# Issuing the second of two output stores from ScalarE's queue instead of SyncE's

## The chip, the core and the metric

The kernel runs on one core of one Trainium2 chip. A core has TensorE (PE), VectorE (DVE), ScalarE (ACT), GpSimd (POOL) and SyncE (SP), and 16 DMA engines that all issuing queues share. The metric is the device time of one execution in microseconds (us), given as the median of several runs. The profile of one execution has its own clock, the span, which is about 1.7 us shorter than the device time. Times "at" some point are counted from the start of the span. The issue of a DMA is the time that its DMA instruction takes on an engine's queue; its landing is the last of the semaphore updates (a semaphore is a counter by which one unit tells another that something is done) that tell of its completion. All runs compared here are of the fast state, with a granted TensorE clock of 0.996 to 1.0.

## The reference

It is one block of grouped-query attention with a K and V cache, followed by the output projection:

```python
B, Sq, D = 32, 4, 1024
Hq, Hkv, Sk, Dh = 32, 4, 2048, 128
q = (x @ wq).reshape(B, Sq, Hq, Dh).transpose(0, 2, 1, 3)
k = repeat(k_cache, Hq // Hkv, axis=1); v = repeat(v_cache, Hq // Hkv, axis=1)
p = softmax(einsum("bhqd,bhkd->bhqk", q, k) * Dh ** -0.5)
o = einsum("bhqk,bhkd->bhqd", p, v)
y = o.transpose(0, 2, 1, 3).reshape(B, Sq, Hq * Dh) @ wo      # all bf16
```

The output y is 128 rows (B times Sq) of 1024 bf16 values, 256 KB. The inputs are 151 MB, 134 MB of them K and V.

## The kernel before

SyncE issues every load, far ahead. The last inputs to arrive are pieces of wo. TensorE multiplies with them into three column ranges of y in PSUM. VectorE and ScalarE evict these ranges to SBUF (the array `y_sb`), and two DMAs of 128 KB store the halves of y.

```python
NA = 512
NB = 800
COLS = ((0, 0, NA), (512, NA, NB), (1024, NB, D))      # (column in PSUM, first, last column of y)
# ... cut ...
        def oproj_out():
            def copy(eng, at, n0, n1, j):
                dst, src = y_sb[:, n0:n1], ps_s[:, at:at + n1 - n0]
                # ScalarE: activation(Copy), VectorE: tensor_copy; both wait for ("op", j), signal ("oe", j)
                # ... cut ...
            for j, eng in enumerate(("dve", "act", "dve")):
                copy(eng, *COLS[j], j)
            for j, (n0, n1, waits) in enumerate(((0, NA, (0,)), (NA, D, (1, 2)))):
                p.dma("sp", lambda e, n0=n0, n1=n1: e.dma_start(out_flat[:, n0:n1], y_sb[:, n0:n1]),
                      [("oe", i) for i in waits], ("out", j), f"s_o{j}")
# ... cut: the projection's matmuls; oproj_out() comes last ...
        p.op("sp", lambda e: None, [("out", j) for j in range(2)])     # SyncE waits for both stores
```

Store 1 (columns 0 to 512) needs VectorE's first eviction. Store 2 (columns 512 to 1024) needs ScalarE's eviction (512 to 800) and VectorE's second (800 to 1024). The first load of the program is x, and the loads of wq follow it on the same queue:

```python
        p.dma("sp", lambda e: e.dma_start(x_sb, x_flat[:, :]), [], "x", "s_x")
        for c in range(4):
            p.dma("sp", ...  w_sb[:, 2 * c:2 * c + 2, :] <- wq_v ...)
```

## Time and profile before

| | |
|---|---|
| device time, median of 3 runs | 363.12 us (363.08 to 363.22) |
| span of the profiled run | 361.4 us |
| busy share: PE, DVE, ACT | 85%, 75%, 28% |
| DMA over the span | 420 GB/s |

The first fence is from the page of the kernel before: in 40 equal slices of the span, the busy tenths of the 16 DMA engines and what they moved.

```profile
DMA  8999999999999999999999999999999999999995
GB/s 321 433 435 432 424 424 428 435 423 424 423 428 432 428 424 430 431 430 426 424 433 428 425 428 430 430 428 426 428 432 432 426 423 435 428 426 428 413 415 215
```

The DMA engines are at nine tenths or more from the second slice to the last but one. The loads set the pace, and the engines fall idle only at the two ends.

The second fence is the timeline of the last microseconds before the change (start, duration, engine, line, operation, tiles, count; in brackets the idle time before it and its releaser). SPq is SyncE's queue issuing a DMA.

```profile
358.04 1.04 DVE L434 CAST P_sb<-ps_s 128x512 bf16<-128x512 f32 x2 [15.34 <-PE ps_s L420]
...
358.59 0.41 ACT L432 ACTIVATE P_sb<-ps_s 128x288 bf16<-128x288 f32 x1 [16.23 <-PE ps_s L420]
358.76 0.82 SPq L439 DMA_DIRECT2D out_dram<-P_sb  x2
```

VectorE's two evictions are merged into one line, and so are SyncE's two issues. (P_sb is the memory that `y_sb` lives in.) The trace's record of the single issues gives their durations, 0.347 and 0.356 us:

```profile
L439 SPq DMA_DIRECT2D out_dram<-P_sb x2: 347/352/356, 358.8 to 359.2; - x2
```

The view of DMA busy share by window shows what the stores do to the engines (columns: busy of PE, PEld, DVE, ACT and POOL, the granted clock, DMA share, GB/s). The window is from the first packet of store 1 to the last of store 2:

```profile
359.60:360.62 1.02, 0.00 (x0) 0.00 (x0) 0.00 (x0) 0.00 (x0) 0.00 (x0) 1.00 0.77 257
```

In the last 3.4 us, no packet of a load runs any more (the last ended 0.29 us before the first eviction began). In these the data of store 2 become ready at 359.093 (semaphore records), and SyncE issues it at 359.225, after store 1.

### The profile page before, as it was taken

How to read it: one execution, taken by the hardware profiler on the slowest of the kernel's cores; microseconds unless marked ns; L12 is line 12 of the kernel's file. 1: busy time of each engine (PE TensorE's matmuls, PEld its weight loads, DVE VectorE, ACT ScalarE, POOL GpSimd, SP SyncE). 2: the span in 40 equal slices, each digit the busy share in tenths (PEclk: the TensorE clock that was granted, in tenths of full speed). 3: DMA queues.
4: the chain of work that ended last, by engine and by line, in shares of the span. 5: the costliest groups of instructions: out<-in, count | busy, mean ns of one | idle time of the engine just before them, and what ended most of it. 6: DMA issues, size and time to landing. Idle time of an engine off the chain costs nothing. (4 is left out here: it accounts for less than half of the span.)

```text
span 361.4 us, 6252 instructions
## 1 busy us (share of the span) xinstructions
PE 307.8 (85%) x3034; PEld 147.0 (41%) x2340; DVE 269.4 (75%) x171; ACT 102.6 (28%) x110; POOL 165.4 (46%) x262
## 2 busy tenths in 40 slices
PE   1988788999989999988999888888888898889896
PEld 1002000444444555444444444443333444449711
DVE  0018799999899888879999888888888888866501
ACT  1014222333333333333333333323222233333000
POOL 8002055255555555554455444445555554444000
PEclk9999999999999999999999999999999999999999
DMA  8999999999999999999999999999999999999995
GB/s 321 433 435 432 424 424 428 435 423 424 423 428 432 428 424 430 431 430 426 424 433 428 425 428 430 430 428 426 428 432 432 426 423 435 428 426 428 413 415 215
DMA packets 12251, 151.66 MB, mean 420 GB/s; under 512 B 1360, under 2 KB 2128, under 8 KB 2768
## 3 DMA queue, kind: packets, MB, share of 16 engines
q1 hardware_dynamic: 12240, 151.52, 99.0%
q8 instruction: 6, 0.10, 0.1%
q14 instruction: 5, 0.04, 0.0%
HBM read 151.26 MB, written 0.26 MB: 419 GB/s over the span
## 5 line engine op out<-in xcount | busy, mean ns | idle before, releaser
L328 DVE STREAM_TRANSPOSE KT_sb<-big 128x2048 f32<-128x2048 f32 x64 | 146.6, 2293 | 16.7 <-DMA big<-in_k_cache_dram 16.7
L354 ACT ACTIVATE P_sb<-ps_s,negmx 128x2048 bf16<-128x2048 f32 x32 | 82.1, 2565 | 185.0 <-DVE negmx L350 185.0
L16 PE MATMUL ps_s<-KT_sb,QD_sb 128*128 128x512 bf16 x384 | 103.7, 377 | 0.0
L385 POOL COPY PD_sb<-PT_sb 32x1024 f32<-32x1024 f32 x62 | 64.1, 1034 | 63.3 <-PE ps_r L394 60.4
L385 POOL COPY big<-PT_sb 32x1024 f32<-32x1024 f32 x61 | 63.1, 1034 | 59.1 <-PE ps_r L394 56.3
L350 DVE TENSOR_REDUCE negmx<-ps_s 128x1 f32<-128x2048 f32 x32 | 73.2, 2286 | 12.4 <-PE ps_s L16 10.7
L394 PE MATMUL ps_r<-big 128*128 128x128 bf16 x1024 | 59.8, 219 | 11.4 <-PEq L85 11.4
L394 PE MATMUL ps_r<-big,PD_sb 128*128 128x128 bf16 x1024 | 59.8, 219 | 9.9 <-PEq L85 9.8
L394 PEld LDWEIGHTS ps_r<-big 128*128 128x128 bf16 x1024 | 57.9, 98 | 22.1 <-issue 21.6
L394 PEld LDWEIGHTS ps_r<-big,PD_sb 128*128 128x128 bf16 x1024 | 58.0, 98 | 21.1 <-issue 20.6
L341 PE MATMUL ps_s<-KT_sb,QD_sb 128*128 128x512 bf16 x128 | 48.3, 377 | 18.4 <-PEq L85 18.4
L341 PEld LDWEIGHTS ps_s<-KT_sb,QD_sb 128*128 128x128 bf16 x128 | 12.3, 96 | 103.1 <-issue 103.1
L363 DVE STREAM_TRANSPOSE PT_sb<-P_sb 128x1024 f32<-128x1024 f32 x32 | 39.8, 1245 | 15.8 <-ACT P_sb L354 15.8
L318 POOL COPY QD_sb<-QT_sb 32x64 f32<-32x64 f32 x128 | 29.4, 230 | 46.2 <-DVE QT_sb L297 20.5
L16 PE MATMUL ps_r<-ident 128*128 128x384 bf16 x173 | 33.3, 325 | 0.0
L366 PEld LDWEIGHTS ps_r<-ssum,permf 128*128 128x128 f32 x64 | 11.9, 187 | 24.8 <-issue 23.1
L403 ACT ACTIVATE QT_sb<-ps_r,rinv 128x128 bf16<-128x128 f32 x32 | 11.8, 367 | 29.4 <-PE ps_r L394 27.2
L279 DVE TENSOR_SCALAR KT_sb<-ps_r 128x512 bf16<-128x512 f32 x2 | 1.3, 684 | 20.3 <-PE ps_r L263 20.3
L420 PE MATMUL ps_s<-big,KT_sb 128*128 128x512 bf16 (+1 forms) x34 | 12.5, 375 | 2.0 <-DMA big<-in_wo_dram 1.2
L434 DVE CAST P_sb<-ps_s 128x512 bf16<-128x512 f32 (+1 forms) x2 | 1.0, 542 | 15.3 <-PE ps_s L420 15.3
L16 PE MATMUL ps_s<-big,KT_sb 128*128 128x224 bf16 (+1 forms) x62 | 12.0, 272 | 0.0
L252 PE MATMUL ps_r<-ident 128*128 128x384 bf16 x32 | 10.3, 322 | 0.0
(41 smaller groups left out, 85.8 us busy)
## 6 DMA issues: line engine op xcount, KB each, us to landing
big<-in_k_cache_dram SPq DMA_DIRECT2D x32, 2048.0 KB, 18.6
big<-in_v_cache_dram SPq DMA_DIRECT2D x32, 2048.0 KB, 22.1
big<-in_wq_dram SPq DMA_DIRECT2D x4, 2048.0 KB, 14.0
big<-in_wo_dram SPq DMA_DIRECT2D x6, 1024.0 KB, 22.8
big<-in_wo_dram SPq DMA_DIRECT2D x2, 512.0 KB, 24.3
big<-in_wo_dram SPq DMA_DIRECT2D x2, 256.0 KB, 22.6
big<-in_wo_dram SPq DMA_DIRECT2D x4, 128.0 KB, 17.5
P_sb<-in_x_dram SPq DMA_DIRECT2D x1, 256.0 KB, 2.6
```

The lines of the kernel that those rows point to most:

```text
L16: return eng.add_instruction(mybir.InstMatmult(name=nc.get_next_instruction_name(), engine=eng.engine, start_tensor_calc=start, stop_tenso ...
L318: p.op("pool", lambda e, s=src, d=dst: e.tensor_copy(d, s), waits if g == 0 else [("pt", i - 2)] * (g == 1 and i > 1), ("qd", i) if g == G ...
L328: p.op("dve", lambda e, s=src, d=dst: e.transpose(d, s), waits, ("kt", i, c), gives="t_kt" if c else None)
L341: mm = lambda e, a_=(out_, lhsT, rhs), f=first, l=last: e.matmul(a_[0], lhsT=a_[1], rhs=a_[2], start=f, stop=l, skip_group_check=True)
L350: p.op("dve", lambda e: e.tensor_reduce(negmx[:, i % 4:i % 4 + 1], ps_s[:, :], AX.X, ALU.max, negate=True), [("qk", i)], ("negmx", i))
L354: p.op("act", lambda e: e.activation(P_sb[:, :, :, :].rearrange("p t r w -> p t w r"), ps_s[:, :].rearrange("p (t w r) -> p t w r", w=2, r=R),
L363: p.op("dve", lambda e: e.transpose(dst, src), [("exp", i)], ("pt", i))
L366: p.op("pe", lambda e: e.matmul(ring[(i if i == L else i // 2 * 2) % 4][:, 510 + i % 2:511 + i % 2], lhsT=permf[:, :], rhs=ssum[:, i % 4:i ...
L385: p.op("dve" if i >= B - 2 and g < i - B + 4 else "pool", lambda e, s=src, d=dst: e.tensor_copy(d, s), [free] * (g == 0 or i >= B - 2) + [ ...
L394: p.op("pe", lambda e: e.matmul(buf[:, 0:Dh], lhsT=pd_of(i)[:, t // 2, :, :, :, t % 2].rearrange("p x g q -> p (x g q)"), rhs=big[:, slot_ ...
L403: p.op("act", lambda e: e.activation(dst, src, ACT.Copy, scale=rinv[:, i % 4:i % 4 + 1]), [("pv", i), ("rinv", i)], ("o", i))
L420: mm = lambda e, a=(out_, lhsT, rhs): e.matmul(a[0], lhsT=a[1], rhs=a[2], start=(u == 0), stop=(u == Hq - 1), skip_group_check=True)
```

## The change

The intent is that SyncE's queue need not finish issuing store 1 before store 2 goes out: ScalarE, which has nothing left to do, issues store 2.

```diff
             for j, (n0, n1, waits) in enumerate(((0, NA, (0,)), (NA, D, (1, 2)))):
-                p.dma("sp", lambda e, n0=n0, n1=n1: e.dma_start(out_flat[:, n0:n1], y_sb[:, n0:n1]),
+                p.dma(("sp", "act")[j], lambda e, n0=n0, n1=n1: e.dma_start(out_flat[:, n0:n1], y_sb[:, n0:n1]),
                       [("oe", i) for i in waits], ("out", j), f"s_o{j}")
```

## The prediction

> **What bounds the kernel.** The page's row of the slices has DMA busy at 9 tenths in all 40 slices but the first and the last, at 421 to 435 GB/s through the middle, while VectorE is busy 75%, ScalarE 28%. Loads of K, V and wo set the pace; after them comes a serial tail. The chain of waits puts 27.84 us on the wo loads, then matmuls, then VectorE's two evictions (358.04, 1.04 us for both). The change touches only what follows them, some 2.6 us of 361.4 (0.7%). SyncE loses one DMA instruction, ScalarE gains it as its last; no other engine's order changes.
>
> **The tail in the trace before** (timeline and semaphore records, us from the span's start): VectorE's first eviction 358.04 to 358.73; SyncE issues store 1 at 358.757 for 0.347; ScalarE's eviction of columns 512 to 800 signals at 359.015; VectorE's second eviction (columns 800 to 1024, 0.392 us) signals at 359.093. SyncE is still issuing store 1 until 359.104, takes its wait at 359.156 and issues store 2 at 359.225 for 0.356. Packets of store 1 run 359.605 to 360.12, those of store 2 360.085 to 360.61; the landings are complete at 360.476 and 360.965; SyncE leaves its wait at 360.98; the closing barrier takes the rest, to 361.41.
>
> **What the change costs and saves.** Removed from SyncE: one issue of 0.356 us. Added on ScalarE: the same issue, which I estimate at the same 0.35 us from SyncE's 0.347 and 0.356. ScalarE is idle after 359.01. But the 0.356 is not the gain: the data of store 2 are only ready at 359.093, eleven ns before SyncE is done with store 1. Estimate: the wait instruction passes 0.017 us after the signal (as SyncE's did) and the DMA starts 0.069 us after that (359.156 to 359.225 in the trace), so about 359.18 instead of 359.225. The gain is about 0.045 us, all on the last chain, if the path from issue to landing stays at the 1.74 us of store 2. The Trainium skill, "DMA: Bandwidth & Descriptors", section "Issuing engines are not separate DMA queues", says that issuing from several engines only saves the sequencer's time to initiate; the trace agrees as far as it goes: both stores' packets keep the engines at 0.66 to 0.97 busy from 359.75 to 360.5.
>
> Possible costs: this would be ScalarE's first DMA issue in the program, and a second queue with packets of its own. "Perfetto Trace Analysis", section "DMA Instruction — HWDGE (DVE, Sync)", describes a lock on the descriptor generator, waited for inside the profiled issue; store 1's issue is over by 359.104, so I expect no collision. A dearer first issue, or a slower start on a cold queue, would outweigh the gain; SyncE's own first issue took 0.38 us, so I expect little.
>
> **Prediction.** 363.08 us, range 362.6 to 363.9 (wider upwards for the cold queue). Faster by over 2%: 0.005; within 2%: 0.985; slower by over 2%: 0.01.
>
> **What would show each step.** The timeline of SyncE shows one store, ScalarE's shows the other, starting at 359.15 to 359.22 relative to the same evictions, 0.33 to 0.40 us long; a second queue appears among the DMA queues with 128 data packets of 1 KB; the gap from ScalarE's issue to landing is 1.6 to 1.8 us; the last landing to the span's end stays 0.45 us.
>
> **What would make it wrong.** An issue on ScalarE longer than 0.45 us; a first packet on the new queue more than 0.5 us after the issue ends; a longer closing barrier or start because of the second queue; or an overlap of the two stores that stretches both.

## The result, and the profile after

The changed kernel took 363.05 us (median of 6 runs, 362.96 to 363.14). The kernel before took 363.13 us (6 runs, 363.01 to 363.27). The ratio is 0.9997 with a 95% interval of 0.9984 to 1.001. A ratio is the mean time of one kernel's fast runs over that of the other's of the same rounds, so it is not quite the ratio of the medians.

The timeline of the end after the change:

```profile
357.81 1.05 DVE L434 CAST P_sb<-ps_s 128x512 bf16<-128x512 f32 x2 [15.19 <-PE ps_s L420]
...
358.38 0.41 ACT L432 ACTIVATE P_sb<-ps_s 128x288 bf16<-128x288 f32 x1 [16.09 <-PE ps_s L420]
358.53 0.35 SPq L439 DMA_DIRECT2D out_dram<-P_sb  x1
358.95 0.37 ACTq L439 DMA_DIRECT2D out_dram<-P_sb  x1
```

One store is now on ScalarE's queue (ACTq). Its issue lasts 0.37 us, not 0.35. The records of the two issues, and the window from the first packet of store 1 to the last of store 2, are these:

```profile
L439 SPq DMA_DIRECT2D out_dram<-P_sb x1: 348/348/348, 358.5 to 358.5; - x1
L439 ACTq DMA_DIRECT2D out_dram<-P_sb x1: 373/373/373, 359.0 to 359.0; - x1
```

```profile
359.38:360.37 0.99, 0.00 (x0) 0.00 (x0) 0.00 (x0) 0.00 (x0) 0.00 (x0) 1.00 0.79 265
```

On the page after the change the DMA queues have a new member, q10, which holds 144 packets; by the packet records 128 are of data, 1 KB each, and 16 are of 4 bytes:

```profile
q1 hardware_dynamic: 12096, 151.39, 99.0%
...
q10 hardware_dynamic: 144, 0.13, 0.1%
```

The two profiles' spans differ by 0.236 us (361.414 and 361.178), but the first eviction of y already starts 0.225 us earlier in the second one (357.813 instead of 358.038), in work that the change does not touch. That part is not the change's: over all the profiles whose program is the same up to that point, it starts anywhere from 357.74 to 358.32. Therefore the table counts from the start of VectorE's first eviction. The numbers are from the instruction, semaphore and landing records of the traces; "same_kernel" and "again" are further profiles of the kernel before and of the changed kernel.

| us after the start of the first eviction | before | same_kernel | after | again |
|---|---|---|---|---|
| issue of store 1 starts | 0.719 | 0.719 | 0.719 | 0.719 |
| VectorE's second eviction signals | 1.055 | 1.063 | 1.062 | 1.062 |
| issue of store 2 starts | 1.187 | 1.188 | 1.139 | 1.138 |
| duration of that issue | 0.356 | 0.355 | 0.373 | 0.373 |
| from that start to the landing | 1.740 | 1.742 | 1.770 | 1.774 |
| from the landing to the end | 0.449 | 0.450 | 0.456 | 0.456 |
| end of the span | 3.376 | 3.380 | 3.365 | 3.368 |

Store 2 is issued 0.05 us earlier, takes 0.03 us longer to land, and the span closes 0.006 us later after that. What is left is about 0.01 us.

The packet records show where the 0.03 us are spent. From ScalarE's issue of store 2 to its first packet it took 0.895 and 0.893 us (after, again). SyncE's issue of store 2, where its packets can be told apart because store 1 is on another queue, took 0.864, 0.864 and 0.877 us (swap, best and tail_best below). From the first packet to the end of the last it took 0.52 us on ScalarE's queue, and 0.52 to 0.54 on SyncE's; from there to the landing 0.35 us on both. So the loss lies between the start of the issue and the first packet, and most of it is the issue itself (0.373 us; 0.348 for SyncE's issue in swap).

### The profile page after: what moved, and what is told of

The parts are those of the page before. It is cut to its first block, busy times and chain, and to the rows that moved or that the text cites. A ratio compares the mean times of both kernels' runs of the same rounds, so it can differ in the third digit from the quotient of the medians.

```text
span 361.2 us, 6248 instructions
## 1 busy us (share of the span) xinstructions
PE 307.2 (85%) x3030; PEld 147.0 (41%) x2340; DVE 269.4 (75%) x171; ACT 102.6 (28%) x110; POOL 165.4 (46%) x262
```

## The experiments

Four explanations were at stake.

- Theory 1, readiness: store 2 can't go before its data are ready, so moving it saves only the small hold-up behind store 1.
- Rival 2: a slow first use of ScalarE's queue swallows a larger gain.
- Rival 3: the DMA engines' own work on the two stores binds, whoever issues.
- Rival 4: the two issuing queues share one descriptor generator, so one waits for the other.

In the diffs of swap, many_sp and ready_sp the lines taken out are those of the changed kernel; in x_act_only and tail_best they are those of the kernel before. Each call also ran the kernel before on the same chip. Two of its runs were odd (365.55 and 364.61 us) and widen the intervals of the ratios, so differences of 0.1 us are not decided by times; medians are quoted, and the short distances are read from the profiles.

| run | median us | before, same call | first eviction to end, us |
|---|---|---|---|
| again | 363.01 | 363.12 | 3.368 |
| swap | 363.04 | 363.12 | 3.341 |
| many_sp | 366.14 | 363.12 | 6.395 |
| many_act | 364.59 | 363.12 | 4.863 |
| ready_sp | 363.11 | 363.17 | 3.385 |
| ready_act | 363.02 | 363.17 | 3.283 |
| x_act_only | 363.28 | 363.17 | 3.379 |
| best | 363.14 | 363.17 | 3.304 |
| same_kernel | 363.15 | 363.13 | 3.380 |
| tail_best | 363.13 | 363.13 | 3.309 |

### again: the changed kernel once more

There is no edit.

> The changed kernel once more. From the start of VectorE's first eviction of y to the end of the span it took 3.365 us, against 3.376 before the change. Theory 1 (readiness: store 2 may go only when VectorE's second eviction signals, and SyncE was held up only some 0.05 us longer than that) expects the same again, 3.34 to 3.39 us, and a time within 0.15 us of before. Rival 2 (a slow first issue on ScalarE's queue swallows a larger gain) expects ScalarE's issue to landing clearly longer than SyncE's 1.74 us, over 1.9.

It measured 3.368 us, as the first profile's 3.365, and ScalarE's issue to landing was 1.774 us. Rival 2 falls in its large form (it needed over 1.9), but its direction is right: the path through ScalarE's queue is 0.03 us longer than SyncE's 1.74.

### same_kernel: the kernel before against itself

There is no edit.

> The kernel before, unchanged, entered as if it were a change, to see how far two sets of runs of one kernel lie apart. Median within 0.15 us of the other set; first eviction to end of the span 3.36 to 3.39 us (3.376 in the first profile), and ScalarE-free issue to landing of store 2 1.73 to 1.75 us. If the tail itself moves by 0.03 us or more between two profiles of one kernel, the gain of 0.01 us read for the change is not shown.

The unchanged kernel repeats its 3.376 us as 3.380, and its 1.740 us from issue to landing as 1.742. x_act_only, whose end is also the unchanged one, shows 3.379. The changed end reads 3.365 and 3.368. So a gain of about 0.01 us in the tail is repeated, while two sets of runs of one kernel differ by 0.02 us in their medians here and by up to 0.4 us from run to run. The 0.08 us between the medians of the result is therefore not shown to be the change's. The set of again lies on the same side, 0.11 us below its partner, but the tail can supply only 0.01 us of either. Other sets scatter about as much beyond their tails: ready_sp, whose tail is no shorter, lies 0.06 us below, and tail_best, whose tail is 0.07 us shorter, lies level. Why is not shown.

### swap: store 1 from ScalarE, store 2 from SyncE

```diff
-                p.dma(("sp", "act")[j], lambda e, ...
+                p.dma(("act", "sp")[j], lambda e, ...
```

> Store 1 issued by ScalarE, behind its own eviction, and store 2 by SyncE, which then has nothing in front of it. Theory 1 (readiness of store 2 alone decides the end): store 1 issues about 0.33 us later than before but had 0.49 us to spare; store 2 issues 0.05 us earlier; from first eviction to the end 3.30 to 3.37 us. Rival 3 (the DMA engines' packets of the two stores, nearly back to back, decide): both bursts now start together, so about 0.25 us more, 3.55 to 3.7 us. Rival 4 (the two issuing queues share one descriptor generator): one of the two issues lasts 0.5 us or more instead of 0.35.

The timeline of the end in this run, and the records of its two issues:

```profile
357.96 1.06 DVE L434 CAST P_sb<-ps_s 128x512 bf16<-128x512 f32 x2 [15.28 <-PE ps_s L420]
...
358.53 0.41 ACT L432 ACTIVATE P_sb<-ps_s 128x288 bf16<-128x288 f32 x1 [16.19 <-PE ps_s L420]
358.68 0.37 ACTq L439 DMA_DIRECT2D out_dram<-P_sb  x1
359.11 0.35 SPq L439 DMA_DIRECT2D out_dram<-P_sb  x1
```

```profile
L439 ACTq DMA_DIRECT2D out_dram<-P_sb x1: 373/373/373, 358.7 to 358.7; - x1
L439 SPq DMA_DIRECT2D out_dram<-P_sb x1: 348/348/348, 359.1 to 359.1; - x1
```

The end came at 3.341 us, inside theory 1's 3.30 to 3.37. But the test against rival 3 did not take place, because my picture of it was wrong. I had expected store 1 to wait until ScalarE's eviction was over. The timeline shows the issue at 358.68, in the middle of the eviction that runs from 358.53 to 358.94. The Trainium skill says why, in "Perfetto Trace Analysis", section "DVE / Act Engine Instruction (TENSOR_ADD, Activation, etc)": the sequencer pushes such an instruction into a wait queue and is then ready for the next one. This trace agrees: store 1 started 0.724 us after the first eviction began, against 0.719 us on SyncE. An engine in the midst of computing can still issue a DMA at once.

The run also separates the queue from the store. SyncE's issue of store 2 lands in 1.736 us (ScalarE's: 1.770 and 1.774), and ScalarE's issue of store 1 lands in 1.759 us (SyncE's: 1.715 to 1.735 in before, same_kernel, after, again, ready_sp and x_act_only). The extra of some 0.03 us follows ScalarE's queue, whichever store it carries. Its size is not sure: in tail_best SyncE's store 2, too, took 1.762 us. Nor is it settled how much of it is a first use. In many_act ScalarE's later issues are dearer as well (0.442 to 0.452 us, SyncE's 0.416 to 0.433), so it is not only that. But best and tail_best differ only in which queue loads x: where ScalarE's queue had carried x before (best), its issue of store 1 took 0.359 us and its first packet came 0.861 us after the start of the issue; where it had not (tail_best), 0.372 and 0.874. By this one pair, about half of the extra issue time goes with the first use.

### many_sp and many_act: eight stores, one queue or two

The disputed thing, issue time on two queues, is made large: y goes out in 8 DMAs of 16 rows that all wait for all evictions. The result is correct.

```diff
-            for j, (n0, n1, waits) in enumerate(((0, NA, (0,)), (NA, D, (1, 2)))):
-                p.dma(("sp", "act")[j], lambda e, n0=n0, n1=n1: e.dma_start(out_flat[:, n0:n1], y_sb[:, n0:n1]),
-                      [("oe", i) for i in waits], ("out", j), f"s_o{j}")
+            for j in range(8):
+                r0, r1 = 16 * j, 16 * j + 16
+                p.dma(("sp", "sp")[j % 2], lambda e, r0=r0, r1=r1: e.dma_start(out_flat[r0:r1, :], y_sb[r0:r1, :]),
+                      [("oe", i) for i in range(3)], ("out", j), f"s_o{j}")
```

many_act has `("sp", "act")[j % 2]` instead. In both, the wait at the end is for all eight stores.

> y is stored in 8 DMAs of 16 rows, all waiting for all three evictions, all issued by SyncE. SyncE's issues follow each other every 0.47 us in the trace before (issues of wo), so the last starts 3.3 us after the first; from first eviction to the end about 6.1 us (5.7 to 6.5), so about 2.7 us slower than before. All theories expect this; it is the base for the next run.

> The same 8 DMAs, issued in turn by SyncE and ScalarE. If the queues issue independently (theory 1 needs that: issue time is saved where the data are ready), the last starts 1.4 us after the first and the end comes about 4.3 us (4.0 to 4.6) after the first eviction, 1.9 us earlier than with SyncE alone. Rival 4 (shared generator, one issue at a time, 0.35 us each): 5.2 us or more. Rival 2 (a cold ScalarE queue): ScalarE's first issue or its first landing is over 0.3 us longer than SyncE's.

The issues of many_sp, then those of many_act, from the timelines:

```profile
358.88 3.60 SPq L440 DMA_DIRECT2D out_dram<-P_sb  x8
```

```profile
358.95 1.77 SPq L440 DMA_DIRECT2D out_dram<-P_sb  x4
358.96 1.82 ACTq L440 DMA_DIRECT2D out_dram<-P_sb  x4
```

Eight issues take 3.60 us on one queue and 1.82 us on two that run side by side. many_sp's end, 6.395 us, is inside the expected 5.7 to 6.5. Rival 4, as a generator that holds up one whole issue for another, falls: the two first issues start 5 ns apart and last 0.363 and 0.396 us. Issue time is really saved where the data are ready. But the end gained 1.53 us (6.395 to 4.863), less than the 1.9 us expected: 4.863 lies between theory 1's 4.0 to 4.6 and rival 4's 5.2 or more. The last issue starts 1.81 us earlier (2.460 instead of 4.267 us after the first eviction), and then takes 1.933 us to land instead of 1.658. So the second queue gives back 0.28 us after the issue has started; which step does it is not told apart. Rival 2's mark was not reached, though ScalarE's first landing took 1.825 us after its issue and SyncE's 1.656.

These runs also show that the tail counts in full: many_sp's tail is 3.02 us longer than the first profile's, and its time is 366.14 - 363.12 = 3.02 us longer.

### ready_sp and ready_act: readiness taken away

Store 2 sends columns 0 to 512 once more, so its data are ready with store 1's. The second half of the output is wrong on purpose.

```diff
-            for j, (n0, n1, waits) in enumerate(((0, NA, (0,)), (NA, D, (1, 2)))):
-                p.dma(("sp", "act")[j], lambda e, n0=n0, n1=n1: e.dma_start(out_flat[:, n0:n1], y_sb[:, n0:n1]),
+            for j, (n0, n1, waits) in enumerate(((0, NA, (0,)), (NA, D, (0,)))):
+                p.dma(("sp", "sp")[j], lambda e, n0=n0, n1=n1: e.dma_start(out_flat[:, n0:n1], y_sb[:, 0:NA]),
```

ready_act has `("sp", "act")[j]`.

> Store 2 sends columns 0 to 512 of y once more (a wrong second half on purpose), so its data are ready with store 1's; both are issued by SyncE. SyncE's issues follow each other every 0.46 to 0.47 us, which is where store 2 stood before, so all theories expect about 3.38 us (3.33 to 3.43) from the first eviction to the end, as before. Base for the next run.

> The same with ScalarE issuing store 2. If readiness is what kept the change small (theory 1) and nothing else binds, ScalarE's issue starts within 0.03 us of store 1's, some 0.45 us earlier than in the run before, and first eviction to end is about 2.95 us (2.85 to 3.1). If the DMA engines' packets bind as well (rival 3: 16 packets of 46 ns for each engine, 0.74 us, where one store has 0.37), the issue is just as early, but the end comes at 3.15 to 3.35 us, so most of the 0.45 us is not gained.

The timeline of the issues in ready_act, and its window from first to last packet; then that window in ready_sp:

```profile
358.81 0.35 SPq L439 DMA_DIRECT2D out_dram<-P_sb  x1
358.81 0.38 ACTq L439 DMA_DIRECT2D out_dram<-P_sb  x1
```

```profile
359.65:360.56 0.91, 0.00 (x0) 0.00 (x0) 0.00 (x0) 0.00 (x0) 0.00 (x0) 1.00 0.86 288
```

```profile
359.88:360.90 1.02, 0.00 (x0) 0.00 (x0) 0.00 (x0) 0.00 (x0) 0.00 (x0) 1.00 0.77 257
```

With readiness out of the way, ScalarE issues store 2 at 0.724 us after the first eviction and SyncE at 1.110, a lead of 0.386 us. The end gains 0.102 us (3.385 to 3.283), about a quarter of it. This is what rival 3 expected (3.15 to 3.35 us). The two stores' packets take 1.02 us at a DMA share of 0.77 when they are issued one after the other, and 0.91 us at 0.86 when issued together: there was little idle engine time to fill (0.23 us, by the 0.77). That the engines' work is what binds is read from these shares; no run changed it by itself. Store 1 pays: its landing moves from 2.451 to 2.648 us. The first packet of store 2 comes 0.215 us behind that of store 1 although the issues start 4 ns apart; whether that is the engines or a step between issue and engines is not told apart here.

So theory 1 is right that readiness held store 2 back, and incomplete: behind it most of the lead is lost between issue and landing, as the shared work of the DMA engines would have it. The Trainium skill states the sharing in "DMA: Bandwidth & Descriptors", section "Issuing engines are not separate DMA queues": issuing from several engines "will only save the time on the sequencer it takes to initiate the DMA". The trace agrees, and adds that even of that saving three quarters can be lost, 0.28 of 0.386 us.

### x_act_only: a second queue at the other end of the kernel

The two stores are on SyncE, as before, but x is loaded by ScalarE, so that SyncE starts the large loads of wq 0.44 us earlier.

```diff
-        p.dma("sp", lambda e: e.dma_start(x_sb, x_flat[:, :]), [], "x", "s_x")
+        p.dma("act", lambda e: e.dma_start(x_sb, x_flat[:, :]), [], "x", "s_x")
```

> The kernel before, both stores on SyncE, but the first load of all, x, issued by ScalarE. SyncE then starts the 8 MB of wq at 0.73 us instead of 1.17. If that issue is on the path of the loads that fill the DMA engines to the end, the DMA engines' idle share from 1.70 to 2.50 us (0.69 busy, so 0.25 us) can be gained: 0.15 to 0.4 us shorter, 362.7 to 363.0 us. If x's own packets delay wq's by as much, or a later wait takes it up, under 0.1 us: 363.05 to 363.2. A cold first issue on ScalarE would show as an issue over 0.5 us or a landing over 3.2 us after it.

The lines of the DMA issues on the page before, and the issues of the first 12 us in this run:

```profile
big<-in_wq_dram SPq DMA_DIRECT2D x4, 2048.0 KB, 14.0
...
P_sb<-in_x_dram SPq DMA_DIRECT2D x1, 256.0 KB, 2.6
```

```profile
big<-in_wq_dram SPq DMA_DIRECT2D x4, 2048.0 KB, 14.6
...
P_sb<-in_x_dram ACTq DMA_DIRECT2D x1, 256.0 KB, 8.2
```

The windows of the start, before and in this run:

```profile
1.70:2.50 0.80, 0.00 (x0) 0.00 (x0) 0.00 (x0) 0.31 (x1) 0.68 (x3) 1.00 0.69 205
2.50:5.00 2.50, 1.07 (x8) 0.82 (x8) 0.53 (x1) 0.00 (x0) 2.44 (x2) 1.00 1.16 439
```

```profile
1.70:2.50 0.80, 0.00 (x0) 0.00 (x0) 0.00 (x0) 0.74 (x1) 0.68 (x3) 1.00 1.43 328
2.50:5.00 2.50, 0.00 (x0) 0.00 (x0) 0.00 (x0) 0.00 (x0) 2.44 (x2) 1.00 0.92 369
```

It was no faster: 363.28 us against 363.17, which is above both expected ranges, by less than times can decide here. SyncE did start wq at 0.73 instead of 1.17 us, but the last piece of wq landed at 23.39 us; in two profiles that load x from SyncE it landed at 23.26 (before) and 23.14 (again). The engines moved more from 1.70 to 2.50 us (328 GB/s, before 205) and less from 2.50 to 5.00 (369, before 439), so the idle share I had hoped to fill did not turn into bytes earlier in the sum. And x, 256 KB, took 8.2 us to land instead of 2.6. The Trainium skill, "DMA: Bandwidth & Descriptors", section "Queues, rings and completion order", says that each DMA engine takes turns between its queues, a packet at a time. The trace agrees as to the turns, though not as to the 9 to 17 descriptors that the page calls typical for a packet: its packet records fit turns of a single record, each of an engine's 8 records of x (2 KB, 84 ns) waiting out one of wq (16 KB, 611 ns). That makes an estimate of 8 x 0.695 = 5.6 us from the first to the last packet of x, and the records start from 2.55 to 8.22 us, in their later part 0.687 us apart again and again. (The records don't name the engine, so the turns are read from the distances.) Issue on ScalarE lasted 0.397 us, against SyncE's 0.381: no cold start here either. The other mark that I had set for a cold start, a landing more than 3.2 us after the issue, was passed; 5.7 of the 8.2 us lie between the first and the last packet of x, where the turns are, and the 1.82 us from the issue to its first packet are not taken apart (SyncE's x before: 1.04).

### best and tail_best: a version that could beat both

best has store 1 and x on ScalarE, store 2 on SyncE, and moves a boundary of the evictions so that ScalarE and VectorE finish together. tail_best is the same with x on SyncE. The edit of tail_best against the kernel before:

```diff
-    NB = 800
+    NB = 832
...
-                p.dma("sp", lambda e, ...
+                p.dma(("act", "sp")[j], lambda e, ...
```

> x and store 1 on ScalarE, store 2 on SyncE, and the boundary between ScalarE's and VectorE's evictions moved from column 800 to 832, which I estimate to let VectorE signal 0.03 us earlier (about 1 ns for each column) and ScalarE some 0.03 us later. If the parts add: first eviction to end 3.29 to 3.34 us, and with the start 0.2 to 0.45 us less than before in all, 362.65 to 362.95 us.

> The run called best without its change to the load of x: store 1 on ScalarE, store 2 on SyncE, boundary of the evictions at 832. If the tail's gain stands and the load of x on ScalarE cost about 0.1 us: first eviction to end 3.29 to 3.32 us, and a median 0.05 to 0.2 us below that of the unchanged kernel in the same call. A reading above the unchanged kernel's would say that gains of this size do not show in the time at all.

In the profile both did what was expected of the tail: 3.304 and 3.309 us from the first eviction to the end, against 3.376 to 3.380. VectorE and ScalarE signal 5 and 6 ns apart (78 before), VectorE 0.02 to 0.05 us earlier than in the unchanged kernel. In the device time nothing shows. tail_best has the same median as the kernel before, 363.13 us (ratio 0.9998, interval 0.9985 to 1.0012), and best has 363.14 against 363.17. A tail shorter by 0.07 us is 0.02% of the kernel and drowns in the 0.58 us by which the start of the tail moves between profiles. My expectation of at least 0.05 us in the median failed, and best's 362.65 to 362.95 us with it; no version here is shown to beat the kernel before.

## Why the prediction was right or wrong

The prediction said 363.08 us and "within 2%"; it was 363.05 us. It was right. That the median came within 0.03 us of the figure is luck: the runs of one kernel lie up to 0.4 us apart, and the tail did not gain the 0.045 us that the figure rests on. Point by point:

- What bounds the kernel: right. The DMA engines stay at nine tenths after the change, and the change reaches only the tail. (The prediction's "421" is a misreading: the page before has 423 to 435 GB/s in slices 2 to 37.)
- "SyncE is still issuing store 1" was not taken for the gain; the prediction named the readiness of store 2 as the limit. Right: the issue moved from 1.187 to 1.139 us after the first eviction, 0.048 us; predicted was 0.045.
- "If the path from issue to landing stays at the 1.74 us of store 2": this is the term that was mis-sized. It became 1.770 and 1.774 us. The issue itself is 0.017 us longer (0.373 against 0.356), the first packet comes later by about as much as the landing, and swap shows that the extra goes with ScalarE's queue. With 0.006 us more in the closing, about 0.01 us of the 0.045 us is left. The mechanism was right, the net gain about four times too large, and predicted and measured gain are both far below what the device time resolves. swap, with SyncE carrying store 2, kept most of it: 3.341 us to the end, 0.035 less than before.
- No collision on the generator: right as far as the issues go. The change itself never put two issues at the same time; many_act and ready_act did, and these issues, which start within 5 ns of each other, each last under 0.4 us.
- No costly first issue: right; 0.373 us for the store (estimated: 0.35), and 0.397 us for x in x_act_only.
- Contention of the packets: named only in passing. ready_act shows that it is the next limit. Had the data been ready at once, the change would have gained 0.10 us, not 0.39.

What stays open: why an issue on ScalarE's queue is longer, how much of that is a first use, and whether the 0.215 us between the first packets of two stores issued together is spent in the DMA engines or just ahead of them.

## What to carry to other kernels

Before moving a DMA to another queue, compare two times: when the old queue is free, and when the data are ready. The later of them sets the earliest start, and here they lay 0.01 us apart. A second queue saves issue time alone, and here that was worth more than about 0.1 us only with many small DMAs that were all ready (eight stores: 1.5 us). The bytes still share the same engines: here a small load put beside large ones landed after 8.2 us instead of 2.6. For effects of hundredths of a microsecond, measure from the last common event in the profile and repeat the profile of the unchanged kernel, since the device time will not tell.

## What the Trainium skill lacked or had wrong

- "DMA: Bandwidth & Descriptors", "Issuing engines are not separate DMA queues": it has no number for the time to initiate. Here one issue took 0.347 to 0.356 us after a wait, and back-to-back issues on SyncE followed each other every 0.46 us (eight in 3.60 us); from ScalarE one took 0.359 to 0.396 us after a wait.
- The same section has nothing on the two queues' differing: the same store from ScalarE took 0.03 to 0.04 us longer from issue to landing than from SyncE (1.770 and 1.774 against 1.736 to 1.743 for store 2; but 1.762 from SyncE in tail_best).
- "DMA: Bandwidth & Descriptors", "Queues, rings and completion order", tells of turns packet by packet, but not what that does to a small load beside a large one: x landed after 8.2 instead of 2.6 us.
- "Perfetto Trace Analysis", "DMA Instruction — HWDGE (DVE, Sync)", tells of a descriptor generator that is locked for one sequencer and shared by DVE and Sync, and notes that which two engines share it is a choice of the compiler, with SP and Activation as the usual pair. It has no number for how long one waits. Issues from SyncE and ScalarE that started 4 and 5 ns apart lasted 0.349 and 0.382 us, 0.363 and 0.396 us: at most some 0.02 us above such issues alone (0.347, 0.373 and, in many_sp, 0.361 us). A longer wait is not seen inside the issue; one behind it is not excluded.
